# One more turn for the fourth raw buffer, and block 0's x stored at another chunk

## The chip, the cores and the metric

The kernel runs on one core of one Trainium2 chip. The metric is the device time of one execution in microseconds (us). Three runs of the kernel before took 917.8, 918.83 and 918.33 us, the median is 918.33 us.

## The reference

Retention attention feeds two feed-forward layers:

```python
ret = scores * Dmat                      # scores = q k^T / 8, Dmat = gamma ** (i - j) for i >= j
attn_out = ret @ v                       # 4 x 8 x 576 x 64
x = attn_out.transpose(0, 2, 1, 3).reshape(2304, 512)
h = x @ w_in                             # 512 x 2048
g = where(h >= 1, h, where(h <= -1, 0, (h + 1) ** 2 / 4))
x = g @ w_out                            # 2048 x 512
return ((x @ w_a) * (x @ w_b)) @ w_out2  # d_ff 1536
```

The weights reach the kernel as 64-bit floating-point words, so each weight tile has to be turned into a 32-bit one on the chip before it can be used.

## The kernel before, in words

**Tiling.** The 2304 tokens are cut into 6 blocks of 384. The first layer goes over its 16 chunks of 128 hidden features in three passes. The first pass takes chunks 0 to 3 for block 0 and chunks 0 to 5 for blocks 1 to 5 (GROUPS1, line 25). In the first pass the attention of the 36 units (18 chunks of 128 tokens, two halves of the heads each) runs beside the first layer, units 0 to 5 ahead of block 0, and six further units during every block (lines 903 to 954). One step of the pass is one chunk f of one block: `l1` multiplies x by the `w_in` tile of f (12 matmuls into `ph`), `act1` makes g, and `l2` (line 566) of the step before multiplies g by the `w_out` tile of f (12 matmuls into the four `acc` banks).

**Weights.** A stream of tiles alternates: `w_in` chunk 0, `w_out` chunk 0, `w_in` chunk 1, `w_out` chunk 1 and so on (line 173). In this document tile n is the n-th of that stream, from 0: tile 3 is `w_out` of chunk 1, tile 4 `w_in` of chunk 2, tile 6 `w_in` of chunk 3. Each goes through these steps:

- `load_raw` (line 138) takes a raw buffer of 128 x 512 64-bit words (512 KB) and issues the load, on SyncE's queue (SP) in the first pass. The buffers: three in the pool `rpool` (line 109), and one more, the fourth, in the pool `r2` (`raw2`, line 364), which exists while the attention runs. Lines 139 and 140 decide: with raw_every at 5, loads 4, 9, 14 and so on go to the fourth buffer, the rest go round the other three. After the attention the setting is replaced by another (line 975).
- `convert` (line 145): two ScalarE (ACT) operations (lines 154 and 155), two VectorE (DVE) operations (156 and 159) and one addition (162). For tiles 0 to 11 the addition is on GpSimd (POOL; ON_POOL, line 30). The raw buffer is free after line 162. The result is in one of two `conv` buffers (line 110).
- `split` (line 165): an ACT cast (167) and a DVE subtraction (168) make the high and low part of the weight tile. The `conv` buffer is free after line 168, and then the matmuls of that tile may start.

`weights_to` (line 227) calls these in stream order, and asks for the loads of two tiles ahead (`depth`, line 214).

**Order of the work.** The Python code emits instructions in program order, and a list scheduler orders each engine's queue at build time by a simulated timeline: among instructions whose inputs and buffers are there it takes the one emitted first (or raised by `high_priority`). On the chip each queue then runs strictly in its order. SP's queue carries the loads of the attention's units (line 394), the raw loads (142), the stores of each block's x to DRAM (`xd`, line 963) and the first-pass partial sums (596).

**The store of x.** The other passes read x of a block again, so in the first pass each block's x (1536 KB) is stored to DRAM once, by the statement at line 963, at the block's first chunk. The first read of block 0's copy is emitted at the second chunk of block 5.

Of the kernel before, what the change touches and what calls it, by code (L numbers as in the profile page):

```python
# [83 lines left out]
def retention_ffn_kernel(  # L84
# [24 lines left out]
    rpool = ctx.enter_context(tc.tile_pool(name="raw", bufs=3))  # L109
# [5 lines left out]
    def mm(o, l, r, start, stop, goes_on=False):  # L115
        nc.tensor.matmul(o, l, r, start=start, stop=stop, skip_group_check=goes_on)  # L116
# [3 lines left out]
    @contextmanager  # L120
    def behind():

        with ExitStack() as both:
            for ins in anchor:
                both.enter_context(tc.issue_after(ins.ins))
            yield
# [5 lines left out]
    def row_chunk(w, f):  # L132
        return w[f * P:(f + 1) * P, :].rearrange("p (c f) -> p c f", c=1)

    raw_pools, raw_turn, raw_every = [rpool], [0], [5]
    side = [nc.sync]

    def load_raw(src):
# [53 lines left out]
    class Raws:  # L192
# [11 lines left out]
        def next(self):  # L204
            i = self.taken
            self.fetch_to(i + 1)
            self.taken += 1
            return self.tiles.pop(i)
# [18 lines left out]
    def weights_to(n):  # L227

        while made[0] < min(n, len(stream)):
            if not free():  # L230
                return
            key = stream[made[0]][0]
            for i in (made[0], made[0] + 1):
                if i not in whole and (i == made[0] or i < ON_POOL):
                    whole[i] = convert(raws1.next(), None, nc.gpsimd if i < ON_POOL else None)
            weights[key] = split(whole.pop(made[0]), take(key))
            made[0] += 1
            raws1.more()
            left = len(stream) - made[0]
            if raws2.held and left < depth[0]:  # L240
                raws2.held = left > 0
                raws2.fetch_to(raws2.taken + depth[0] - left)
            left = 2 * GROUPS1[1][0][1] - made[0]
            if depth[0] > 2 and 0 <= left < 3:
                raws2.fetch_to(3 - left)

    def used(key):

        weights.pop(key, None)
        room[home.pop(key)][1] += 1  # L250
# [82 lines left out]
    def make_more(n):  # L333

        if made[0] < n and free() > 2:
            weights_to(made[0] + 1)
        elif free() >= 2:
            next(work, None)
# [169 lines left out]
    def rounds_to(limit):  # L508

        while done[0] < min(limit, NU):  # L510
            i = done[0]
            while loaded[0] < min(max(i + 4, min(i + 8, 12)), NU):
                load_unit(loaded[0])
                loaded[0] += 1
            while ready[0] < min(i + 2, NU):
                prepare(ready[0])
                ready[0] += 1
            while scored[0] < min(i + 2, NU):
                score(scored[0])
                scored[0] += 1  # L520
            output(i)
            done[0] += 1
# [9 lines left out]
    def fetch_x(b, space):  # L532
        t = xpool.tile([P, 2, NCC, TB], F32R, tag="x", name="x")
        nc.sync.dma_start(t.bitcast(F32), space[b])
        return t


    def l1(x, w):
        ph = ps.tile([P, 512], F32, tag="ps", name="ph")
        ops = []  # L540
        for cc in range(NCC):
            ws = slice(cc * P, (cc + 1) * P)
            for a, z in HL:
                ops.append((ph[:, :TB], w[:, a, ws], x[:, z, cc, :]))
        return ph, [(o, l, r, i == 0, i == len(ops) - 1) for i, (o, l, r) in enumerate(ops)]

    def act1(ph):
        t = tpool.tile([P, TB], F32, tag="t", name="t")
        g = gpool.tile([P, 2, TB], F32R, tag="g", name="g")
        nc.scalar.activation(t, ph[:, :TB], AF.Relu, bias=0.5, scale=0.5)  # L550
        nc.scalar.activation(t, t, AF.Square)  # L551
        nc.vector.scalar_tensor_tensor(  # L552
            out=t, in0=t, scalar=1.0, in1=ph[:, :TB], op0=ALU.min, op1=ALU.max
        )
        anchor[:] = [
            nc.scalar.copy(g[:, 0, :], t),  # L556
            nc.vector.tensor_sub(g[:, 1, :], t, g[:, 0, :].bitcast(F32)),  # L557
        ]
        return g
# [6 lines left out]
    def l2(step):  # L566
        i, b, f, first, last = step
        if first:
            ys[i, b] = accs(NCC)
        y, w, g = ys[i, b], weights["o", f], gs.pop(step)  # L570
        for m in range(NCC):
            ws = slice(m * P, (m + 1) * P)
            for n, (a, z) in enumerate(((0, 0), (1, 0), (0, 1))):
                mm(y[m][:, :TB], w[:, a, ws], g[:, z, :], first and n == 0, last and n == 2)
        if last_use[f] == (i, b):
            used(("o", f))
        if last:
            y_out(i, b)
# [3 lines left out]
    def fetch_y(i, b):  # L582
        for m in range(NCC):
            t = yin[b, m] = t2pool.tile([P, TB], F32, tag="t2", name="yin")
            nc.sync.dma_start(t, yd[i - 1][b][:, m, :])
# [293 lines left out]
    first = 2 * P + places * H  # L879
# [40 lines left out]
    def needed(step):  # L920
        return place["o", step[2]] + 1

    credit = 0.0
    for s, step in enumerate(steps):
        i, b, f, first, last = step
        f0, f1 = GROUPS1[i][b]
        busy = i == 0 and b < NB - 1
        if (i, b, first) == (1, NB - 3, True):
            raws2.held = True
        if (i, b) == (1, NB - 3) and f >= f1 - 3:  # L930
            raws1.fetch_to(2 * GROUPS1[1][0][1] + f - f1 + 4)
        if (i, b, first) == (2, NB - 2, True):
            depth[0], raw_every[0], raw_pools[1:] = 2, 5, []
        credit += 0.0 if busy else 1.0 if i == 0 else PACE
        ahead = max(needed(t) for t in steps[s:s + 2 + (not busy)])
        if made[0] < ahead:
            weights_to(ahead)
            credit = 0.0
        while credit >= 1.0:
            with behind() if i == 0 else nullcontext():  # L940
                make_more(2 * GROUPS1[1][0][1] if i == 0 or (i == 1 and b < NB - 2) else len(stream))
            credit -= 1.0
        if first:
            if i == 0:
                x = xt[b]
            else:
                x = xt.pop((i, b)) if (i, b) in xt else fetch_x(b, xd)
        due = min(UPB * (b + 1) + -(-(f - f0 + 1) * UPB // (f1 - f0)), NU) if i == 0 else NU
        ph, ops = l1(x, weights["i", f])
        for half in (ops[:6], ops[6:]):  # L950
            for o in half:
                mm(*o)
            with tc.high_priority(60):
                rounds_to(min(done[0] + 1, due))
        assert done[0] == due
        if last_use[f] == (i, b):
            used(("i", f))
        gs[step] = act1(ph)
        if prev:
            l2(prev)  # L960
        prev = step
        if i == 0 and first:
            nc.sync.dma_start(xd[b], x.bitcast(F32))
        if i == 0 and done[0] == NU and stage is None:
            att.close()
            del raw_pools[1:]
            t2pool = ctx.enter_context(tc.tile_pool(name="t2", bufs=8))
            txpool = ctx.enter_context(tc.tile_pool(name="tx", bufs=5))
            bpool = ctx.enter_context(tc.tile_pool(name="b", bufs=1))
            side[0] = nc.gpsimd  # L970
            room["wx"] = [ctx.enter_context(tc.tile_pool(name="wx", bufs=WBUFS2)), WBUFS2]
            stage = first_sb.enter_context(tc.tile_pool(name="stage", bufs=1))
            rx = ExitStack()
            raw_pools += [rx.enter_context(tc.tile_pool(name="rawx", bufs=3))]
            depth[0], raw_every[0] = 4, 2
        if i > 0 and first:
            fetch_y(i, b)
        if i == 2 and b == 3 and first:
            load_y(0)
        if i == 2 and b == NB - 1 and first:  # L980
            making = right(0)
        if i == 2 and b == NB - 1:
            for _ in range(1 + (not first)):
                next(making, None)
        if f == f0 + 1:
            ni, nb = (i, b + 1) if b + 1 < NB else (i + 1, 0)
            if 0 < ni < 3:
                xt[ni, nb] = fetch_x(nb, xd)
        if i == 2 and b == NB - 1:
            load_to(9)  # L990
# [13 lines left out]
    for n in range(NSB):  # L1004
# [3 lines left out]
        for p in range(NF2 // 2):  # L1008
            for w in range(2):
# [11 lines left out]
                if quad:  # L1021
# [5 lines left out]
                    else:  # L1027
                        act2(other, quad)
                        f = 2 * quad.at[1]
# [73 lines left out]
```

## Time and profile before

| | us |
|---|---|
| median of three runs | 918.33 |
| the profiled execution, own time | 918.67 |
| its span, first to last instruction | 916.9 |
| outside the span | 1.8 |
| TensorE (PE) busy in the span | 905.0 (99%) |
| DVE busy | 654.9 (71%) |
| ACT busy | 486.2 (53%) |
| POOL busy | 88.0 (10%) |

The span runs from the first to the last instruction on the slowest (here the only) core, and times in the rows below are counted from its start. The prediction is summed against the profiled execution and then set beside the median.

### The profile page before, as it was taken

How to read it: one execution, taken by the hardware profiler on the slowest of the kernel's cores; microseconds unless marked ns; L12 is line 12 of the kernel's file. 1: busy time of each engine (PE TensorE's matmuls, PEld its weight loads, DVE VectorE, ACT ScalarE, POOL GpSimd, SP SyncE). 2: the span in 40 equal slices, each digit the busy share in tenths (PEclk: the TensorE clock that was granted, in tenths of full speed). 3: DMA queues.
4: the chain of work that ended last, by engine and by line, in shares of the span. 5: the costliest groups of instructions: out<-in, count | busy, mean ns of one | idle time of the engine just before them, and what ended most of it. 6: DMA issues, size and time to landing. Idle time of an engine off the chain costs nothing.

```text
span 916.9 us, 14681 instructions
## 1 busy us (share of the span) xinstructions
PE 905.0 (99%) x5324; PEld 896.7 (98%) x5324; DVE 654.9 (71%) x1230; ACT 486.2 (53%) x961; POOL 88.0 (10%) x116
## 2 busy tenths in 40 slices
PE   8999999999999999999999999999999999999998
PEld 7898999999999999999999999999999999999998
DVE  6889788887899985789956877675454486155365
ACT  2566466565887775677735555553333254233243
POOL 3442111100221110011000000000000000000000
PEclk9999999999999999999999999999999999999999
DMA  9976445241899996799994998888854489956484
GB/s 353 358 222 250 162 140 192 87 162 57 280 328 336 405 385 221 258 354 388 393 401 134 372 412 282 283 291 284 311 198 161 147 272 386 365 192 224 162 271 169
DMA packets 82007, 244.13 MB, mean 266 GB/s; under 512 B 8432, under 2 KB 36208, under 8 KB 79632
## 3 DMA queue, kind: packets, MB, share of 16 engines
q1 hardware_dynamic: 72864, 210.01, 63.6%
q0 software_dynamic: 8928, 33.03, 10.3%
q8 instruction: 42, 0.69, 0.3%
q14 instruction: 29, 0.24, 0.1%
q10 hardware_dynamic: 144, 0.17, 0.1%
HBM read 181.83 MB, written 61.34 MB: 265 GB/s over the span
## 4 chain that ended last, share of the span: by engine, by line
PE 94%; DVE 3%; DMA 1%; issue 1%; SPq 0%; ACT 0%; POOL 0%; POOLq 0%
PE acc L116 32%; PE ph L116 21%; PE qx L116 16%; PE qy L116 8%; PE po L116 5%; PE late L116 4%; PE qz L116 4%; PE s L116 2%; PE pn L116 2%; DMA con<-in_const 1%; DVE conv L159 1%; DVE xf L496 0%; DVE w L168 0%; DVE z L411 0%; DVE retf L432 0%
## 5 line engine op out<-in xcount | busy, mean ns | idle before, releaser
L116 PE MATMUL acc<-g,w 128*128 128x384 f32 x1296 | 250.9, 336 | 2.0 <-ACT w L167 1.1
L116 PEld LDWEIGHTS acc<-g,w 128*128 128x128 f32 x1296 | 226.8, 188 | 2.8 <-ACT w L167 1.4
L116 PE MATMUL ph<-x,w 128*128 128x384 f32 x1152 | 219.3, 336 | 0.0
L116 PEld LDWEIGHTS ph<-x,w 128*128 128x128 f32 x1152 | 200.6, 188 | 0.1
L116 PE MATMUL qx<-tx,w 128*128 128x384 f32 x864 | 165.5, 334 | 0.0
L116 PEld LDWEIGHTS qx<-tx,w 128*128 128x128 f32 x864 | 151.2, 188 | 0.0
L672 ACT COPY keep<-qx 128x384 f32<-128x384 f32 x126 | 60.2, 481 | 139.3 <-PE qx L116 133.9
L116 PE MATMUL qy<-tx,w 128*128 128x384 f32 x432 | 86.6, 334 | 0.0
L550 ACT ACTIVATE t<-ph 128x384 f32<-128x384 f32 x96 | 46.9, 489 | 64.5 <-PE ph L116 61.6
L116 PE MATMUL acc<-sp,w 128*128 128x384 f32 x432 | 77.5, 334 | 0.0
L116 PEld LDWEIGHTS qy<-tx,w 128*128 128x128 f32 x432 | 75.9, 188 | 0.0
L116 PEld LDWEIGHTS acc<-sp,w 128*128 128x128 f32 x432 | 75.1, 188 | 0.0
L552 DVE SCALAR_TENSOR_TENSOR t<-t,ph 128x384 f32<-128x384 f32 x96 | 52.5, 549 | 23.7 <-ACT t L551 23.0
L556 ACT CAST g<-t 128x384 fp32r<-128x384 f32 x96 | 48.9, 511 | 35.5 <-DVE t L552 31.9
L557 DVE TENSOR_TENSOR g<-t,g 128x384 fp32r<-128x384 f32 x96 | 53.3, 556 | 16.4 <-ACT g L556 16.2
L765 DVE TENSOR_TENSOR sp<-gb,sp 128x768 fp32r<-128x768 f32 x42 | 40.2, 956 | 22.2 <-ACT sp L764 21.9
L764 ACT CAST sp<-gb 128x768 fp32r<-128x768 f32 x42 | 35.2, 837 | 32.6 <-PE acc L116 18.8
L155 ACT ACTIVATE raw<-raw 128x512 int32<-128x512 uint32 x68 | 45.7, 675 | 11.3 <-DMA raw<-in_moe_w_a 5.4
L551 ACT ACTIVATE t<-t 128x384 f32<-128x384 f32 x96 | 50.5, 526 | 1.6
L707 DVE TENSOR_TENSOR keep<-keep 128x384 f32<-128x384 f32 x36 | 20.1, 557 | 40.8 <-ACT keep L672 40.8
L116 PE MATMUL qz<-tx,w 128*128 128x384 f32 x216 | 43.4, 334 | 0.0
L694 DVE TENSOR_TENSOR keep<-qz,keep 128x384 f32<-128x384 f32 x36 | 20.0, 556 | 29.8 <-PE qz L116 28.8
(117 smaller groups left out, 1222.3 us busy)
## 6 DMA issues: line engine op xcount, KB each, us to landing
w<-q SPq DMA_DIRECT2D x126, 512.0 KB, 5.6
q<-q SPq DMA_DIRECT2D x42, 512.0 KB, 7.6
w<-o SPq DMA_DIRECT2D x42, 512.0 KB, 4.8
u<-in_qkv SPq DMA_DIRECT2D x32, 640.0 KB, 4.8
x<-xd SPq DMA_DIRECT2D x12, 1536.0 KB, 9.1
raw<-in_moe_w_out POOLq DMA_DIRECT2D x21, 512.0 KB, 7.5
xd<-x SPq DMA_DIRECT2D x6, 1536.0 KB, 8.0
yin<-y SPq DMA_DIRECT2D x48, 192.0 KB, 6.2
```

Of the source, the lines that this page charges most:

```text
L116: nc.tensor.matmul(o, l, r, start=start, stop=stop, skip_group_check=goes_on)
L155: nc.scalar.activation(r, low, AF.Copy, scale=2.0 ** -29)
L550: nc.scalar.activation(t, ph[:, :TB], AF.Relu, bias=0.5, scale=0.5)
L551: nc.scalar.activation(t, t, AF.Square)
L552: nc.vector.scalar_tensor_tensor(out=t, in0=t, scalar=1.0, in1=ph[:, :TB], op0=ALU.min, op1=ALU.max)
L556: nc.scalar.copy(g[:, 0, :], t),
L557: nc.vector.tensor_sub(g[:, 1, :], t, g[:, 0, :].bitcast(F32)),
L672: nc.scalar.copy(t, o[:, :HT])
L694: nc.vector.tensor_add(self.c11, z[:, :HT], self.c11)
L707: nc.vector.tensor_add(self.c22, self.c22, self.s5)
L764: nc.scalar.copy(t[:, 0], b)
L765: nc.vector.tensor_sub(t[:, 1], b, t[:, 0].bitcast(F32))
```

## The change

raw_every is 4 instead of 5 at the start, so that loads 3, 7, 11 go to the fourth buffer instead of loads 4 and 9. The store of x is emitted at the first chunk of its block as before for blocks 1 to 5, and at the third chunk (f = 2) for block 0.

```diff
-    raw_pools, raw_turn, raw_every = [rpool], [0], [5]
+    raw_pools, raw_turn, raw_every = [rpool], [0], [4]
...
         if prev:
             l2(prev)
         prev = step
-        if i == 0 and first:
+        if i == 0 and f == f0 + (2 if b == 0 else 0):
             nc.sync.dma_start(xd[b], x.bitcast(F32))
```

## Rows read from the trace of the kernel before

**Rows 1.** The page, part 1: busy time of each engine.

```profile
PE 905.0 (99%) x5324; PEld 896.7 (98%) x5324; DVE 654.9 (71%) x1230; ACT 486.2 (53%) x961; POOL 88.0 (10%) x116
```

**Rows 2.** Table of stretches: length, busy PE, PEld, DVE, ACT, POOL, PEclk, DMA, GB/s.

```profile
40.00:60.00 20.00, 18.33 (x93) 17.05 (x93) 17.35 (x33) 13.49 (x26) 9.61 (x9) 0.91 0.70 231
```

**Rows 3.** Waits of PE over the span: total us, times, longest.

```profile
PE acc L116 <- ACT w L167: 1.1, 1, 1.1
PE acc L116 <- DVE w L168: 0.9, 1, 0.9
```

**Rows 4.** The table of stretches again, two short ones.

```profile
43.00:44.00 1.00, 1.00 (x5) 1.00 (x4) 0.63 (x2) 1.00 (x3) 0.00 (x0) 0.50 0.93 360
...
70.00:75.00 5.00, 3.48 (x18) 2.62 (x18) 4.92 (x11) 1.77 (x5) 1.74 (x2) 1.00 0.99 396
```

**Rows 5.** PE's timeline, 38 to 55 us: start, us, operation, count.

```profile
38.40 1.29 PE L116 MATMUL acc<-g,w 128*128 128x384 f32 x6
40.77 0.98 PE L116 MATMUL acc<-g,w 128*128 128x384 f32 x4 [1.08 <-ACT w L167]
42.65 2.68 PE L116 MATMUL acc<-g,w 128*128 128x384 f32 x8 [0.90 <-DVE w L168]
45.13 0.53 PE L116 MATMUL ph<-x,w 128*128 128x384 f32 x1
...
46.78 0.59 PE L116 MATMUL po<-retf,u 128*128 128x256 f32 x2
...
53.42 2.33 PE L116 MATMUL ph<-x,w 128*128 128x384 f32 x12
```

**Rows 6.** SP's queue, 13 to 31 us: DMA issues.

```profile
13.80 2.96 SPq L142 DMA_DIRECT2D raw<-in_moe_w_in  x1
...
21.28 2.71 SPq L142 DMA_DIRECT2D raw<-in_moe_w_out  x2
27.42 0.33 SPq L963 DMA_DIRECT2D xd<-x  x1
30.03 0.38 SPq L142 DMA_DIRECT2D raw<-in_moe_w_in  x1
```

**Rows 7.** DMA issues begun at 13.80, 21.28, 27.42, 30.03; last figure us to landing.

```profile
raw<-in_moe_w_in SPq DMA_DIRECT2D x1, 512.0 KB, 12.0
...
raw<-in_moe_w_out SPq DMA_DIRECT2D x1, 512.0 KB, 13.6
...
xd<-x SPq DMA_DIRECT2D x1, 1536.0 KB, 12.5
...
raw<-in_moe_w_in SPq DMA_DIRECT2D x1, 512.0 KB, 11.1
```

**Rows 8.** POOL's timeline: two conversion additions and a raw load.

```profile
18.59 1.36 POOL L162 TENSOR_TENSOR conv<-conv,raw 128x512 int32<-128x512 int32 x1 [0.86 <-issue]
...
40.75 1.30 POOL L162 TENSOR_TENSOR conv<-conv,raw 128x512 int32<-128x512 int32 x1 [0.68 <-DVE conv L159]
...
79.40 0.92 POOL L142 DMA_DIRECT2D raw<-in_moe_w_in  x1 [4.18 <-issue]
```

**Rows 9.** ACT's timeline: first operation of a conversion, tiles 2, 3 and 6.

```profile
26.35 0.67 ACT L154 ACTIVATE conv<-raw 128x512 f32<-128x512 f32 x1
...
35.98 0.65 ACT L154 ACTIVATE conv<-raw 128x512 f32<-128x512 f32 x1
...
45.12 0.68 ACT L154 ACTIVATE conv<-raw 128x512 f32<-128x512 f32 x1 [0.71 <-DVE w L168]
```

**Rows 10.** DVE's timeline: last operation of a weight tile, tiles 2, 3, 4 and 6.

```profile
30.69 0.69 DVE L168 TENSOR_TENSOR w<-conv,w 128x512 fp32r<-128x512 f32 x1 [0.40 <-ACT w L167]
...
40.99 1.61 DVE L168 TENSOR_TENSOR w<-conv,w 128x512 fp32r<-128x512 f32 x1
...
44.40 0.69 DVE L168 TENSOR_TENSOR w<-conv,w 128x512 fp32r<-128x512 f32 x1
...
52.74 0.69 DVE L168 TENSOR_TENSOR w<-conv,w 128x512 fp32r<-128x512 f32 x1
```

## The prediction, made before the changed kernel was run

> **What bounds the kernel now.** First the busy shares: PE is busy for 905.0 of 916.9 us [rows 1], so the whole change can win at most the 12 us in which PE is idle, plus what a lowered clock costs. The raw buffers matter only while the first tiles are made, so I read the table of stretches for the start: between 40 and 60 us PE is busy for 18.33 of 20 us and its mean granted clock is 0.91 [rows 2]. That is a stall with a slow restart. The list of PE's waits says for what: 1.1 us for the ACT half and 0.9 us for the DVE half of a weight tile, once each [rows 3]. PE's timeline places both [rows 5]: after six `acc` matmuls that end at 38.40 + 1.29 = 39.69 come 12 `acc` matmuls with tile 3, four from 40.77 (after 1.08 us of waiting) and eight from 42.65 (after 0.90). Then the first matmul with tile 4 starts at 45.13. The clock explains the rest: at 43 to 44 us it is granted at 0.50, the 1.2 GHz level, after that idle time [rows 4], and the eight `acc` matmuls take 2.68 us, where six took 1.29.
>
> DVE's rows show why the tiles were late. Tile 3 is ready at 40.99 + 1.61 = 42.60, tile 4 at 44.40 + 0.69 = 45.09 [rows 10], 40 ns before PE starts on it. So two late tiles follow each other, and PE at full clock would have met the second wait too. Tile 6 repeats it: ready at 52.74 + 0.69 = 53.43, and PE starts on it at 53.42 [rows 5, 10].
>
> Why is tile 3 late? Its load is the first of the two issued from 21.28, because it needs the buffer of tile 0, which POOL frees at 18.59 + 1.36 = 19.95, and it lands at 21.28 + 13.6 = 34.9 [rows 6 to 8]. Tile 4 had the fourth buffer, went ahead of it at 13.80 and landed at 25.8 [rows 6, 7], but is wanted after it and is converted after it. The spare buffer is given to the tile that can't use it. I give ACT's conversion at 35.98 to tile 3 because tiles are converted in stream order; it starts 1.1 us after the landing [rows 9]. From the first ACT operation to the end of the split the chain takes 26.35 to 31.38 = 5.0 us for tile 2, 35.98 to 42.60 = 6.6 for tile 3, and 45.12 to 53.43 = 8.3 for tile 6 [rows 9, 10].
>
> **The change, part by part.** No instruction is added or removed; two loads trade places and one store is emitted later.
>
> *Tile 3 gets the fourth buffer.* It should be issued where tile 4's load now is, 13.80, and land at about 25.8. With 5.0 to 8.3 us of conversion it is ready between 31 and 35 us, against 39.69 when PE wants it. The 2.0 us of waiting go. The conversion has to fit on ACT, DVE and POOL about ten microseconds earlier, and the same work is then missing from them later.
>
> *Tile 4 takes tile 3's old buffer.* It is issued at 21.28 and lands at 34.9, nine microseconds later than now, and this is what is late next. Tile 3's place at 35.98 on ACT is free for it. Its chain is bounded by the rows: 34.9 + 5.0 = 39.9 at best, 35.98 + 8.3 = 44.3 at worst. I take tile 3's own 6.6 us, since it runs in the same place among the same neighbours: ready at 42.6, which is 2.5 us before today's 45.09.
>
> *What PE makes of it.* At full clock 12 `acc` matmuls take at most twice the 1.29 us of six, so from 39.69 they end by 42.3, and PE waits 0.3 us for tile 4. The five matmuls between 45.13 and 46.78 ran mostly at half clock, so they take about 0.83 us at full clock. PE would reach at 43.4 what it reaches today at 46.78: 3.3 us won. That the clock stays up I take from 70 to 75 us, where PE idles 1.5 us in pieces and 1.00 is granted [rows 4].
>
> *Tile 6 takes some back.* A conversion needs one of two `conv` buffers. Tile 6's begins at 45.12 though it landed at 30.03 + 11.1 = 41.1; it waits for tile 4's split to end at 45.09 [rows 6, 7, 9]. With tile 4 ready at 42.6 it starts there, and after 8.3 us is ready at 50.9. PE would want it at 53.42 - 3.3 = 50.1 and waits 0.8. So 2.5 us remain, the time that tile 4 came forward. Bounds: 0.8 us if tile 4's chain takes 8.3, and 46.78 - 39.69 - 2.58 - 0.83 = 3.7 if both tiles are on time.
>
> *Later tiles.* Tiles 7 and 11 take the fourth buffer instead of 9. From tile 5 on a tile waits for a `conv` buffer rather than its load, so I cost this at nothing; the cover is that wait, and should it go, a 512 KB load shows, some 1.3 us by the spacing of landings (xd at 39.9, tile 6 at 41.1 [rows 6, 7]).
>
> *The store.* It leaves SP at 27.42, when x is ready, and lands at 39.9 [rows 6, 7]. Emission only decides among ready instructions: a raw load of tile 14, emitted after block 4 of the first pass, left POOL at 79.40, though block 0's third chunk only began at 45.13 and the four blocks after it can't have been over [rows 5, 8]. So I expect the store still near 27 us, with nothing queued behind it but tile 6's load at 30.03. Cost: none. If it did move to the third chunk, tile 6 would land up to 3.7 us earlier (1536 KB at about 415 GB/s), which the `conv` wait hides, and its bytes would pass at 40 to 60 us, where the DMA engines are 0.70 busy [rows 2]. Unit loads that queue behind it there would come up to 3.7 us late, and I keep nothing to 3.7 us as its ends.
>
> *A shared resource.* Tile 3's split on DVE took 1.61 us beside a POOL addition (40.75 to 42.05) where the others took 0.69 [rows 8, 10]: it lost 0.92 us there. The Trainium skill says why (SBUF — State Buffer, on the port pair that DVE and GpSimd share): an instruction that reads two SBUF inputs is fully blocked while a GpSimd operation holds the pair. The row agrees. By that rule, as an estimate, an earlier POOL addition blocks DVE at about 30 us for up to its whole 1.3 us. My sum leaves this out, since the same blocking leaves 38 to 42 us.
>
> *The sum.* 918.67 (the profiled execution: span 916.9 and 1.8 around it) - 2.5 = 916.2. The median of the runs is 0.34 lower, so 915.8 us.
>
> **The rivals.** *Little is won.* Tile 4's chain stretches to 8.3 us, or tile 3's addition at about 30 us blocks DVE for 1.3 us in front of attention work that PE needs, or the scheduler leaves the conversions in their places and nothing moves. Gains of 0.8, 1.2 and 0, or 917.5, 917.1 and 918.3 us. For it: DVE is the tightest engine beside PE (17.35 of 20 us [rows 2]). Against it: tile 4's load lands before 35.98 either way, and a delay of PE before 42 us is partly absorbed by the wait for tile 4. The blocking is the page's rule just named. This is 0.32.
>
> *Slower: tile 4 falls behind the store.* SP runs in order. If tile 4's load is not placed at 21.28 but after x's store, as tile 6's is at 30.03, it lands at 41.1 and is ready at 41.1 + 6.6 = 47.7, 2.6 us later than today; tile 6 passes this on, and the clock stays down as it does today. 918.3 + 2.6 = 920.9 us. It decides once tile 4 lands after 45.09 + 1.84 - 6.6 = 40.3. For it: tile 4 has lost its free buffer. Against it: its new buffer is free at 19.95, long before x is ready. 0.13.
>
> *The store doesn't move* is likely, as said, and changes none of these numbers.
>
> **How the numbers follow.** 0.2% of 918.3, or 1.84 us, is about what a measurement of this kernel can tell from no change. The forecast, a gain from 1.84 to 3.7 us, has 0.55; it is the only case of faster. Little won is 0.32, within 0.2%, and the slower rival 0.13. The likeliest case runs from 914.6 to 916.5 by itself. The range goes down to 914.2 (both tiles on time, and some of the store's room) and up over all of little won to 919.4, part of the unit loads' 3.7 us against the gain; above it lies most of the slower rival, and below little.
>
> **What would show it.** In the changed profile: SP issues a `w_out` load near 13.8 us and a `w_in` load near 21.3; ACT's conversion of tile 3 starts before 31 us; the two PE waits on `w` near 40 us are gone or under 1 us; the granted clock at 43 to 44 us is 1.00; tile 4's split ends near 42.6 and tile 6's near 50.9; the store is still near 27 us. I am wrong if tile 4's split ends no earlier than 44.5, if the clock falls all the same, if PE's idle time near 70 us grows by what was won at 40, or if the queues' order after 120 us brings new waits.

## The result, and the profile after

The changed kernel takes 924.65 us (median of six runs, 923.95 to 928.68) against 918.07 us for the kernel before beside it: a ratio of 1.0074, 95% interval 1.0054 to 1.0093. It is 6.6 us slower, where 2.5 us less was forecast. A seventh execution on record, not in the median, took 922.66 us. The profiled execution took 928.68 us with a span of 926.8 us; it is the longest of the six, and what follows explains part of that.

The busy shares of the changed kernel, and the table of stretches for the start (the columns are those of [rows 2]), first of the changed kernel, then two rows of the kernel before:

```profile
PE 908.8 (98%) x5324; PEld 899.7 (97%) x5324; DVE 659.7 (71%) x1230; ACT 485.0 (52%) x961; POOL 85.3 (9%) x116
```

```profile
20.00:40.00 20.00, 17.40 (x85) 15.67 (x84) 18.79 (x33) 8.37 (x17) 8.40 (x11) 0.91 1.04 401
40.00:60.00 20.00, 18.85 (x107) 17.46 (x106) 19.22 (x33) 12.56 (x24) 7.80 (x6) 1.00 0.62 196
60.00:80.00 20.00, 16.92 (x91) 15.65 (x90) 19.83 (x33) 12.17 (x22) 10.97 (x9) 0.94 0.83 300
```

```profile
20.00:40.00 20.00, 19.69 (x110) 18.09 (x108) 18.05 (x40) 10.30 (x20) 9.02 (x11) 1.00 1.00 383
...
60.00:80.00 20.00, 18.48 (x106) 17.10 (x105) 17.85 (x33) 10.22 (x20) 6.66 (x6) 1.00 0.92 329
```

The same 1230 DVE instructions are busy for 659.7 us instead of 654.9 [rows 1]. Between 60 and 80 us DVE is busy for 19.83 of 20 us with 33 instructions, where the same number took 17.85 before. PE's busy time is 2.3 us lower from 20 to 40 us and 1.6 us lower from 60 to 80. From 40 to 60 us, where the kernel before lost its time [rows 2], PE has gained half a microsecond.

SP's queue did what was predicted. Tile 3's load starts at 13.75, tile 4's at 21.23, and the store of x leaves at 27.33, where it was [rows 6]:

```profile
13.75 2.95 SPq L142 DMA_DIRECT2D raw<-in_moe_w_out  x1
...
21.23 0.38 SPq L142 DMA_DIRECT2D raw<-in_moe_w_in  x1
...
27.33 0.33 SPq L963 DMA_DIRECT2D xd<-x  x1
```

The waits of PE for the weight tiles [rows 3] are gone from its list. Three others stand in the same stretch, of which the kernel before has only that for line 552, with 0.9 us:

```profile
PE pn L116 <- DVE t L552: 2.9, 1, 2.9
...
PE ph L116 <- DVE retf L432: 1.9, 1, 1.9
...
PE ph L116 <- ACT raw L155: 1.1, 1, 1.1
```

The first of them in time is the wait for `retf`. PE's timeline has it at the second chunk, which started at 32.66 before (the start of the 12 `ph` matmuls of a chunk is used as a landmark below) and starts at 35.67 now:

```profile
35.67 3.50 PE L116 MATMUL ph<-x,w 128*128 128x384 f32 x12 [1.90 <-DVE retf L432]
...
78.12 1.23 PE L116 MATMUL pn<-u 128*128 128x128 f32 x4 [2.88 <-DVE t L552]
```

DVE's timeline just before it, POOL's beside it, and then three rows of POOL's timeline in the kernel before:

```profile
28.74 1.71 DVE L159 SCALAR_TENSOR_TENSOR conv<-raw,conv 128x512 uint32<-128x512 uint32 x1
...
31.59 3.33 DVE L168 TENSOR_TENSOR w<-conv,w 128x512 fp32r<-128x512 f32 x1
34.85 0.68 DVE L432 TENSOR_TENSOR retf<-s,con 128x512 f32<-128x512 f32 x1
```

```profile
28.59 1.30 POOL L162 TENSOR_TENSOR conv<-conv,raw 128x512 int32<-128x512 int32 x1 [4.48 <-DVE conv L159]
29.85 1.06 POOL L402 TENSOR_TENSOR u<-u,con 128x256 f32<-128x256 f32 x1
30.86 0.30 POOL L405 MEMSET u<- 64x256 f32 x1
31.13 1.28 POOL L162 TENSOR_TENSOR conv<-conv,raw 128x512 int32<-128x512 int32 x1
32.38 0.60 POOL L402 TENSOR_TENSOR u<-u,con 128x256 f32<-128x256 f32 x1
32.93 0.30 POOL L405 MEMSET u<- 64x256 f32 x1
33.20 1.17 POOL L402 TENSOR_TENSOR u<-u,con 128x256 f32<-128x256 f32 x2
```

```profile
29.95 0.81 POOL L402 TENSOR_TENSOR u<-u,con 128x256 f32<-128x256 f32 x1
30.70 0.30 POOL L405 MEMSET u<- 64x256 f32 x1
30.97 0.88 POOL L402 TENSOR_TENSOR u<-u,con 128x256 f32<-128x256 f32 x1
```

Read them against each other. Tile 2's split on DVE takes 0.69 us alone [rows 10]. It starts at 31.59, while POOL is in tile 3's addition, the one that the early load brought forward to 31.13. POOL then goes on without a gap until 34.37 (lines 402 and 405 prepare the attention's units), and the split ends 0.55 us after that, at 34.92. So the split's record lasts through the rest of the addition and four more POOL instructions. In the kernel before it started at 30.69 [rows 10], when POOL was at the end of a preparation and about to begin a memset; it took 0.69 us, and it was POOL's next preparation that took 0.88 us, where one alone took 0.60 (the profile's times for POOL are rough). Tile 3's early conversion brought a second, smaller delay just ahead: its operation of line 159 at 28.74 met tile 2's addition and took 1.71 us instead of 0.69. `retf`, for which PE waits, is next in DVE's queue after the split. The profile counts the whole 3.33 us as busy time of DVE.

DVE was held beside POOL again and again. To measure it, I summed for the DVE instructions begun from 20 to 80 us what each took beyond the median of its line and operation, counting excesses over 0.1 us. In the kernel before this is 2.6 us in 7 instructions, in the changed one 10.4 us in 11. Every one of these instructions overlaps a POOL instruction. In the changed kernel ten of the eleven end 0.3 to 0.6 us after the first POOL instruction that they met; only the split at 31.59 lasts through several.

The third wait of PE in the list stands at 55.20, before its first matmuls with tile 6. Tile 4's conversion did not go the way of the forecast either. Its first operation on ACT and its split on DVE:

```profile
40.16 0.65 ACT L154 ACTIVATE conv<-raw 128x512 f32<-128x512 f32 x1
```

```profile
46.48 0.69 DVE L168 TENSOR_TENSOR w<-conv,w 128x512 fp32r<-128x512 f32 x1
```

It starts at 40.16 instead of 35.98 and is split at 47.17 instead of 42.6.

Finally the clock, in the table of stretches of the changed kernel:

```profile
38.00:40.00 2.00, 2.00 (x7) 1.82 (x7) 1.04 (x3) 0.90 (x3) 0.00 (x0) 0.53 1.05 399
...
78.00:80.00 2.00, 1.88 (x7) 1.88 (x8) 1.99 (x5) 1.13 (x2) 0.07 (x1) 0.50 0.85 291
```

After each of the two long waits it is granted at or near 0.50, the 1.2 GHz level, as after the stall of the kernel before [rows 4].

### The profile page after: what moved, and what is told of

Read it like the earlier page. It is cut to its first block, busy times and chain, and to the rows that moved or that the text cites. A ratio compares the mean times of both kernels' runs of the same rounds, so it can differ in the third digit from the quotient of the medians.

```text
span 926.8 us, 14695 instructions
## 1 busy us (share of the span) xinstructions
PE 908.8 (98%) x5324; PEld 899.7 (97%) x5324; DVE 659.7 (71%) x1230; ACT 485.0 (52%) x961; POOL 85.3 (9%) x116
## 4 chain that ended last, share of the span: by engine, by line
PE 84%; DVE 8%; DMA 5%; issue 1%; ACT 1%; SPq 0%; POOL 0%; POOLq 0%; DVEq 0%; ACTq 0%
PE acc L116 28%; PE ph L116 17%; PE qx L116 16%; PE qy L116 8%; PE late L116 4%; PE qz L116 4%; PE po L116 3%; DMA raw<-in_moe_w_a 2%; PE s L116 2%; PE pn L116 1%; DMA con<-in_const 1%; DVE w L168 1%; DVE xf L496 1%; DVE conv L159 1%; DMA raw<-in_moe_w_b 1%
## 5 line engine op out<-in xcount | busy, mean ns | idle before, releaser
L116 PE MATMUL ph<-x,w 128*128 128x384 f32 x1152 | 222.7, 338 | 3.0 <-DVE retf L432 1.9
L116 PEld LDWEIGHTS ph<-x,w 128*128 128x128 f32 x1152 | 203.3, 190 | 3.8 <-issue 2.1
L557 DVE TENSOR_TENSOR g<-t,g 128x384 fp32r<-128x384 f32 x96 | 53.2, 556 | 11.0 <-ACT g L556 10.1
L285 DVE TENSOR_TENSOR q<-stage,q 128x256 fp32r<-128x256 f32 x84 | 33.0, 424 | 14.3 <-ACT q L284 14.2
```

Source lines behind the costliest of these rows:

```text
L285: nc.vector.tensor_sub(lo, st[:, o], hi.bitcast(F32))
```

## The experiments

Each kernel was run beside the kernel before, whose median was 917.24 us in experiments 1 to 4, 917.22 in 5 to 8, and 917.08 in 9 to 12. "Excess" is the sum over DVE's instructions just defined, "second chunk" is PE's landmark (32.66 before). Of these 63 executions of the kernel before, 15 had a mean granted clock of 0.998 and took 918.28 to 919.12 us; the other 48 had 0.999 or 1.000 and took 916.80 to 917.99. The execution that the prediction was summed against (918.67 us, with the clock at 0.50 near 43 us) is like the 15.

| | median us | ratio, 95% interval | excess us | second chunk |
|---|---|---|---|---|
| 1 store alone | 918.33 | 1.0002 (0.9993 to 1.0012) | 3.4 | 32.52 |
| 2 buffers alone | 922.1 | 1.0049 (1.0033 to 1.0066) | 10.7 | 35.77 |
| 3 loads 3, 9 | 922.5 | 1.0053 (1.0038 to 1.0068) | 9.7 | 35.64 |
| 4 loads 4, 7, 11 | 919.04 | 1.0022 (1.0012 to 1.0032) | 5.3 | 32.71 |
| 5 changed kernel again | 924.2 | 1.0068 (1.0049 to 1.0087) | 10.7 | 35.82 |
| 6 tile 3 held | 917.14 | 0.9994 (0.9985 to 1.0004) | 5.6 | 32.73 |
| 7 tile 3's addition on DVE | 921.58 | 1.0045 (1.003 to 1.006) | 8.6 | 34.71 |
| 8 all additions on DVE | 917.54 | 1.0001 (0.9991 to 1.001) | 1.7 | 34.12 |
| 9 before, all on DVE | 919.77 | 1.0029 (1.0018 to 1.004) | 1.3 | 33.44 |
| 10 tiles 8 to 11 on DVE | 922.5 | 1.0062 (1.0049 to 1.0075) | 8.0 | 35.56 |
| 11 held, all on DVE | 919.63 | 1.0021 (1.0012 to 1.003) | 2.1 | 33.62 |
| 12 held, 8 to 11 on DVE | 915.55 | 0.9981 (0.9973 to 0.999) | 4.4 | 32.76 |

### 1 and 2: the two parts alone

```diff
# 1, on the kernel before
-        if i == 0 and first:
+        if i == 0 and f == f0 + (2 if b == 0 else 0):
# 2, on the kernel before
-    raw_pools, raw_turn, raw_every = [rpool], [0], [5]
+    raw_pools, raw_turn, raw_every = [rpool], [0], [4]
```

> The store's edit alone, on the kernel before. Theory A (the store is taken by SP when x is ready, wherever it is emitted, so this part does nothing): the store leaves SP near 27.4 us as before, the time is 918 us within 1 us. Rival S (the store moves into the time of the unit loads and costs part of the 6.6 us): over 920 us, the store after 40 us.

> The raw buffers' edit alone, on the kernel before. Theory A (all of the loss comes from the buffers): 924.5 us within 1 us, with a DVE split of over 3 us near 31.6 us. Rival S (the store has a part in it): under 922 us.

The store's part does nothing: in the profile of experiment 1 every engine runs the same instructions in the same order as before, and the store leaves SP where it did:

```profile
27.28 0.33 SPq L963 DMA_DIRECT2D xd<-x  x1
```

The loss is in the buffers. Experiment 2 lost 4.9 us, less than the 924.5 us that theory A gave, though its queues are the changed kernel's instruction for instruction. Its profile has the same three waits of PE, 2.9, 1.9 and 1.2 us. What differs in the first 100 us is the clock. The same two stretches in experiment 2:

```profile
38.00:40.00 2.00, 2.00 (x12) 1.90 (x11) 1.97 (x5) 1.97 (x5) 0.00 (x0) 1.00 1.04 398
...
78.00:80.00 2.00, 2.00 (x13) 2.00 (x12) 1.92 (x6) 1.42 (x3) 0.00 (x0) 1.00 1.00 299
```

The count of matmuls says it too: 12 here and 7 in the changed kernel's profile in the same two microseconds. So the lowered clock is a part of the loss of its own, which some executions have and others don't. It is not the whole difference between the two profiles (926.8 and 920.0 us): the changed kernel's also waits 1.8 us for g and 0.7 us for line 595 between 405 and 450 us, where experiment 2's waits 0.3 us in all.

### 3 and 4: the first exchange, and the later ones

```diff
# 3, on the kernel before; in 4 the loads are (4, 7, 11)
-        r = raw_pools[-1] if raw_turn[0] % raw_every[0] == raw_every[0] - 1 else rpool
+        r = raw_pools[-1] if (raw_turn[0] in (3, 9) if side[0] is nc.sync else
+            raw_turn[0] % raw_every[0] == raw_every[0] - 1) else rpool
```

> On the kernel before, loads 3 and 9 take the fourth buffer instead of 4 and 9: only the first exchange of the change. Theory P (tile 3's early addition on POOL meets DVE's split of tile 2 and holds it up, which sets the rest back): most of the loss is here, 922 to 925 us, the split near 31.6 us takes over 2 us. Rival L (the later loads 7 and 11 in the fourth buffer spoil the stretch from 54 to 85 us): 916 to 919 us, since tiles 3 and 4 are then the only ones moved.

> On the kernel before, loads 4, 7 and 11 take the fourth buffer: the first exchange is left out and only the later ones are made. Theory P: 917 to 919 us, no split over 2 us near 31 us. Rival L: 921 to 925 us, with PE's wait for DVE of 2 to 3 us near 75 us.

The exchange of tiles 3 and 4 alone gives as much as the loss of experiment 2, and tile 2's split is held up as before. DVE's groups by line from 28 to 36 us in experiment 3:

```profile
L168 DVE TENSOR_TENSOR w<-conv,w 128x512 fp32r<-128x512 f32 x1 | 3.3, 3335 | 0.0
```

The later loads alone cost a little, 0.04 us more than theory P allowed. Experiment 4 is also worth a look for a reading of mine. In its profile the old stall is there (1.08 and 0.92 us of waiting for w), but the clock stays at 1.00. PE starts on tile 4 at 44.20, before tile 4's split has begun on DVE:

```profile
44.20 0.34 PE L116 MATMUL ph<-x,w 128*128 128x384 f32 x1
...
45.24 0.59 PE L116 MATMUL po<-retf,u 128*128 128x256 f32 x2
...
51.86 2.33 PE L116 MATMUL ph<-x,w 128*128 128x384 f32 x12
```

```profile
44.47 0.69 DVE L168 TENSOR_TENSOR w<-conv,w 128x512 fp32r<-128x512 f32 x1
```

### 5: the changed kernel again

> The changed kernel once more. The raw buffers' edit alone (922.1 us) has the same order of instructions on every engine, and its profile shows the same PE waits but a granted clock of 1.00 where the changed kernel's shows 0.50 near 38 and 80 us. If those dips come and go with the run: runs from 921.5 to 925 us, with the lower mean clock in the longer ones. If the store's place matters after all: 924 us and above in all.

It took 922.6 to 925.47 us in four runs. With experiment 2, the same order on every engine, that makes eight runs from 921.5 to 925.5 us. The store's place doesn't matter: two of the four lie under 924 us. That the longer runs have the lower clock holds only roughly: 925.27 us came at a mean clock of 0.998 and 923.13 us at 0.997. The profile of this one has both long waits, a clock of 1.00 after the first and a lowered one after the second, and lies between the other two at block 1's third chunk: 78.44 in experiment 2, 79.72 here, 81.06 in the changed kernel's first profile, against 76.28 before.

### 6 and 7: tile 3's addition out of the way

```diff
# 6, on the changed kernel
-                if i not in whole and (i == made[0] or i < ON_POOL):
+                if i not in whole and (i == made[0] or i < ON_POOL and i != 3):
...
-        ahead = max(needed(t) for t in steps[s:s + 2 + (not busy)])
+        ahead = max(needed(t) for t in steps[s:s + 1 + (s > 0) + (not busy)])
+        if s == 1:
+            with behind():
+                weights_to(4)
# 7, on the changed kernel
-nc.gpsimd if i < ON_POOL else None)
+nc.gpsimd if i < ON_POOL and i != 3 else None)
```

> The changed kernel, with tile 3's conversion issued behind the first act1, so that its POOL addition comes after the four unit preparations, not among them; its load stays early. Theory P (the POOL addition at 31 us holds up DVE's split of tile 2): no split over 2 us near 31 us, PE starts the second chunk near 32.7 as in the kernel before, 916 to 919 us. Rival L (tile 4's late load and the later tiles cost the time): 921 us or more, with the PE wait near 75 us as long as in the changed kernel (2.9 us).

> The changed kernel, with tile 3's addition on DVE instead of POOL, early as it is. Theory P: DVE does 0.7 us more work and loses some 2.6 us less to waiting; PE starts the second chunk by 34 us, 917 to 920 us. Rival L: 921 us or more.

Experiment 6 keeps the buffers and the loads of the changed kernel and brings it back to the time before, 7 us below experiment 5. DVE's and POOL's timelines:

```profile
30.73 0.69 DVE L168 TENSOR_TENSOR w<-conv,w 128x512 fp32r<-128x512 f32 x1 [0.40 <-ACT w L167]
```

```profile
33.44 0.61 POOL L402 TENSOR_TENSOR u<-u,con 128x256 f32<-128x256 f32 x1 [0.72 <-DMA u<-in_qkv]
36.42 1.30 POOL L162 TENSOR_TENSOR conv<-conv,raw 128x512 int32<-128x512 int32 x1 [2.37 <-DVE conv L159]
```

Tile 2's split takes 0.69 us again, tile 3's addition comes after the unit preparations, and PE runs the `acc` matmuls of both first chunks without a wait:

```profile
32.73 2.33 PE L116 MATMUL ph<-x,w 128*128 128x384 f32 x12
...
38.47 3.47 PE L116 MATMUL acc<-g,w 128*128 128x384 f32 x18
41.78 0.34 PE L116 MATMUL ph<-x,w 128*128 128x384 f32 x1
```

PE is 3.35 us ahead of the profile of the kernel before at tile 4 (41.78 against 45.13) and 3.2 at tile 6. Against the same start at full clock (44.20 at tile 4 in experiment 4) it is 2.4 us. Tile 4's conversion now begins where the forecast had it, at 36.04, and its split ends at 43.20:

```profile
36.04 0.66 ACT L154 ACTIVATE conv<-raw 128x512 f32<-128x512 f32 x1
```

```profile
42.52 0.68 DVE L168 TENSOR_TENSOR w<-conv,w 128x512 fp32r<-128x512 f32 x1
```

That is the mechanism that was forecast. It didn't last: of the 3.35 us 2.1 are left at 146 us and 0.3 at 500 us, after waits of 0.9 us for a unit's split (line 411), 0.7 for a store's copy and 1.3 for g, which the kernel before doesn't have or has shorter.

Experiment 7 missed: with the addition on DVE the second chunk starts at 34.71, not by 34, and the time, 921.58 us, lies in rival L's range. The custom DVE form of the addition meets the unit preparations on POOL itself:

```profile
31.84 1.52 DVE L162 CUSTOM_DVE_ANT_0 conv<-raw,conv 128x1024 uint16<-128x1024 uint16 x1
...
33.28 0.68 DVE L168 TENSOR_TENSOR w<-conv,w 128x512 fp32r<-128x512 f32 x1
```

One microsecond of the first loss went, the late wait for line 552 (2.8 us) stayed. I read this as two losses, not one; experiment 10 tests it.

### 8 and 9: no addition on POOL, with the new and the old buffers

```diff
# 8 on the changed kernel, 9 on the kernel before
-nc.gpsimd if i < ON_POOL else None)
+None)
```

> The changed kernel, with the additions of all 12 first tiles on DVE. DVE's operations that last longer than their usual time from 20 to 80 us add up to 10.4 us in the changed kernel and 2.6 us in the one before. Theory P: that sum falls to 4 us or less, against some 8 us of additions that DVE now does itself, 919 to 924 us. Rival D (DVE has simply too much to do there, and POOL has no part in it): 8 us more work on DVE give 928 us or more.

> The kernel before (raw_every 5), with the additions of all 12 first tiles on DVE. With the changed buffers this edit gave 917.5 us, 6.7 us less than the changed kernel. Theory P (the buffers' exchange helps by itself and was spoiled by POOL's additions): here tile 3 is late again, with PE waits for w near 40 us, so 918.5 to 921 us, above the 917.5 with the new buffers. Rival N (the exchange is worth nothing even without the collisions): 917 to 918 us.

This is the clearest test. DVE gets 12 additions more, of 0.68 us where one runs undisturbed, in a stretch where it looked full, and the changed kernel becomes 6.7 us faster than experiment 5. From 20 to 80 us, experiment 8:

```profile
20.00:40.00 20.00, 18.90 (x102) 16.90 (x101) 19.73 (x41) 10.08 (x21) 3.99 (x8) 1.00 1.04 402
40.00:60.00 20.00, 19.60 (x113) 18.50 (x112) 19.64 (x42) 13.79 (x26) 2.14 (x3) 1.00 0.72 241
60.00:80.00 20.00, 19.13 (x116) 18.04 (x115) 19.85 (x35) 12.65 (x26) 5.54 (x6) 1.00 0.93 329
```

DVE began 116 instructions in these 60 us, where it began 96 in the changed kernel's first profile. It was busy for 59.2 us against 57.8, and POOL for 11.7 instead of 27.2. The excess fell from 10.7 to 1.7 us. A DVE that simply had too much to do (rival D) would have lost 8 us more. The time is better than theory P allowed (919 us at best). Part of the 6.7 us is the clock, which was at 0.999 or 1.000 in all ten runs; against experiment 2 it is 4.6 us. The move is not free: the second chunk still starts at 34.12.

Experiment 9 does the same to the old buffers and is 2.7 us slower than the kernel before, 919.77 us: there the additions on POOL had held DVE up little (an excess of 2.6 us), and now DVE has the extra work. PE's waits from 35 to 46 us show that tile 3 is late again:

```profile
PE acc L116 <- ACT w L167: 0.8, 1, 0.8
PE acc L116 <- DVE w L168: 0.6, 1, 0.6
```

With the additions off POOL the exchange of the buffers is worth 919.77 - 917.54 = 2.2 us, and the two intervals don't overlap. With them on POOL it costs 5 to 7 us. That the 2.2 us come close to the 2.5 of the forecast is in part luck, as the next section says.

### 10 to 12: the late collisions, and a version that beats both

```diff
# 10, on the changed kernel; 12, on experiment 6
-nc.gpsimd if i < ON_POOL else None)
+nc.gpsimd if i < 8 else None)
# 11, on experiment 6
-nc.gpsimd if i < ON_POOL else None)
+None)
```

> The changed kernel, with the additions of tiles 8 to 11 on DVE and those of 0 to 7 on POOL as they are. Theory P, with two separate losses (the collision at 31 us, 3.1 us there, and the collisions from 60 to 77 us, some 2.6 us at the wait of 2.9 us): the first stays, PE starts the second chunk near 35.7, the second goes, the wait for line 552 near 75 us falls under 1 us, 919 to 922 us. Rival F (the first collision is the whole cause and the late wait only follows from it): 923 us or more, the late wait stays over 2 us.

> The changed kernel with tile 3's conversion held behind the first act1, and the additions of all 12 first tiles on DVE. A try at a version that beats both. Theory P: no collision with additions at all, but DVE is nearly full to 80 us, so 915.5 to 918 us.

> The changed kernel with tile 3's conversion held behind the first act1, and only the additions of tiles 8 to 11 on DVE. Theory P: tile 3 in time without the collision at 31 us, and fewer collisions from 60 to 80 us than with the hold alone (917.1 us): 915 to 917.5 us.

Experiment 10 took away the late wait and left the first collision, as theory P had it and against rival F. DVE's groups from 28 to 36 us, and PE's waits:

```profile
L168 DVE TENSOR_TENSOR w<-conv,w 128x512 fp32r<-128x512 f32 x1 | 3.3, 3340 | 0.0
```

```profile
PE pn L116 <- DVE t L552: 0.8, 2, 0.6
```

At block 1's third chunk it is level with the kernel before, 0.4 us behind. But its time, 922.5 us, is 0.5 above the expected end: 1.3 us came back as a wait of `acc` for a copy on ACT (line 592) that the changed kernel doesn't have. It is also no faster than experiment 2 (922.1 us), which has both losses. The waits were told apart; how much of the total each is worth was not.

Experiment 11 missed its range by 1.6 us. Its profile has a wait of 2.7 us for line 552 again, with DVE busy for 19.85 of 20 us from 60 to 80 us and little excess. That points to the work itself being too much there, which no run shows by itself.

Experiment 12 is the best, 915.55 us, 1.5 us below the kernel before and 8.7 below experiment 5. Its stretches:

```profile
20.00:40.00 20.00, 20.00 (x114) 18.70 (x113) 19.24 (x39) 11.55 (x23) 9.75 (x13) 1.00 1.02 390
40.00:60.00 20.00, 19.49 (x107) 18.05 (x106) 19.69 (x39) 13.93 (x27) 7.32 (x8) 1.00 0.79 287
60.00:80.00 20.00, 18.52 (x111) 17.27 (x110) 19.83 (x36) 11.85 (x24) 4.21 (x6) 1.00 0.85 296
```

PE is 58.0 of 60 us busy here, against 53.2 in the changed kernel, and the 2.9 us that it leads the profile before from 100 us on are kept to the end of the first layer. By the medians 1.5 us are won; that profile was of an execution with the lowered clock.

## Why the prediction was wrong

**Right: which loads move.** Tile 3's load at 13.75, tile 4's at 21.23, the store unmoved, and the waits for w near 40 us gone. The store was rightly costed at nothing (experiment 1).

**Right in kind: what the exchange is worth.** 2.5 us were forecast for tiles 3 and 4 in time; 2.2 us were measured where POOL's additions are gone (experiments 8 and 9), and PE is 2.4 us ahead at tile 4, at equal clock, where only the order was mended (experiment 6). The agreement with 2.5 is in part luck. Of the 3.3 us that PE was to win by 46.78, 1.5 are the lowered clock of that one profile: after the same waits, experiment 4 at full clock is at the same place at 45.24. Most executions of the kernel before don't have that loss, so the change could not win it there.

**Wrong: "The conversion has to fit on ACT, DVE and POOL about ten microseconds earlier, and the same work is then missing from them later."** This is the step that failed. The work was counted as so much time on each engine, and the same time was credited later. But its place matters. At 31 us POOL was in a run of unit preparations, and tile 3's addition was put in the middle of it. Tile 2's split, which before started as a memset began and ran in 0.69 us, now started inside that addition and took 3.33; the operation of line 159 before it took 1.71 instead of 0.69. PE waited 1.9 us for what stood behind the split, started the second chunk 3.0 us later than before, and what the early tile had won was gone. Holding tile 3's conversion back (experiment 6) or taking the additions off POOL (experiment 8) brought the time back to 917.1 and 917.5 us.

**Wrong: "My sum leaves this out, since the same blocking leaves 38 to 42 us."** The blocking was seen in the trace, and the rule of the Trainium skill (SBUF — State Buffer, on the port pair that DVE and GpSimd share) was named beside it. I bounded it by one POOL operation, 1.3 us, once, and the sum has it at nothing. Measured were 2.6 us for that split, through several POOL operations in a row, 1.0 us for the operation of line 159, and 10.4 instead of 2.6 us over 60 us. It did leave 38 to 42 us, but the new order of all queues met POOL in eleven places, against seven before. That rule has the second to start wait until the first is finished; ten of the eleven agree with it, and the split that outlasts five POOL instructions goes beyond it. Why POOL went on there is not shown. The rival that held the blocking was given a gain of 1.2 us, where it decided for a loss.

**Wrong: "Tile 3's place at 35.98 on ACT is free for it."** Tile 4's conversion began at 40.16, behind work on ACT that waited for the delayed second chunk, and its split ended at 47.17. That is past 44.5, which I had named as a sign of being wrong. PE has no wait at tile 4, since it came there late itself. In experiment 6, without the early delay, the place was free (36.04).

**Wrong: the reading of the two dates.** Tile 4's split ends 40 ns before PE starts on it [rows 5, 10], and I took that for a wait. Experiment 4 has the same split at the same time, with the clock at 1.00, and PE starts 0.9 us earlier, before the split has begun. It was the lowered clock that kept PE, and the two dates agreed by chance. PE's first matmul with tile 4 reads only the high part, which ACT writes, so it need not wait for the end of the split; the description of `split` above has this wrong. Tile 6 doesn't show a wait either: PE's row at 53.42 has no idle time before it [rows 5].

**Wrong: "That the clock stays up".** It fell after the waits of 1.9 and 2.9 us in the first profile and not in experiment 2's. How much of the loss this is stays open. The medians of the two, 924.65 and 922.1 us, differ by 2.5 us, but one run of the changed kernel took 924.06 us at a mean clock of 1.000, and runs at 0.998 lie between 922.29 and 925.27. Experiment 2 lost 4.9 us with the clock at 0.998 to 1.000, so most of the loss is not the clock. Which executions are hit was not found out.

**The rival for a slower kernel** had the wrong mechanism. Tile 4 did not fall behind the store.

Left open: how much of the loss each collision makes. Every edit gave a new order of the queues with waits of its own, as experiments 6 and 10 show at 110 us and later, so single collisions could not be taken out with all else kept.

## What to carry to other kernels

Where POOL and DVE work side by side, an instruction that is moved earlier has to be placed against POOL's queue as well as counted: look what POOL runs when a DVE instruction on the critical path is to start, and how long POOL then goes on without a pause. A DVE that seems full may be waiting; set the durations of single instructions against the median of their kind before believing the busy share, and if they exceed it, moving work from POOL to DVE can make the kernel faster, as in experiment 8. Where they hardly do, the same move costs time, as in experiment 9. When a build-time scheduler orders the queues, a change of one buffer can reorder all of them, and the forecast needs a rival for that.

## What the runs showed that was not expected

A DVE instruction was held through the rest of one POOL instruction and four more, 31.59 to 34.37, and not only through the one that it met. All five profiles in which the split starts inside tile 3's addition show it (3.33 or 3.34 us: the changed kernel and experiments 2, 3, 5 and 10). Also a single-input operation was held: line 156, with one SBUF input, took 1.53 us at 43.08 in the changed kernel against 0.42 usually, beside a POOL addition from 42.93 to 44.32.

The same order of instructions on every engine, with the same waits of PE (1.9 and 2.9 us), ran with a granted clock of 0.50 after both, after one or after none of them. Idle time alone did not say whether the clock would fall.
